# A remade order of work and a buffer of its own for batch 0's V, in attention followed by a mixer

## The chip, the cores and the metric

The kernel runs on one core of one Trainium2 chip. The metric is the device time of one execution in microseconds (us); three runs of the kernel before gave 656.35, 661.31 and 663.45, median 661.31.

## The reference

Four batches of eight heads, 576 tokens, head size 64. Queries and keys are rotated by position, scores are softmaxed and weight V; the result, 512 channels wide, goes through a token mixer of rank 32 (U, V of the mixer) and a channel mixer with a hidden width of 2048.

```python
q_rot, k_rot = rotate(q), rotate(k)
scores = q_rot @ k_rot.T / sqrt(64)
attn = exp(scores - max); attn = attn / (sum(attn) + 1e-9)
x = (attn @ v), heads side by side            # (4, 576, 512)
u = x + ((x.T @ U) @ V).T                     # mixes tokens, moe_U 576x32, moe_V 32x576
out = u + relu(u @ w_ch1) @ w_ch2             # 512x2048, 2048x512
```

The inputs come as float32; the kernel is handed the four mixer arrays as 64-bit words and turns them into float32 itself.

## The kernel before, in words

**Who decides the order.** Nothing is issued as the code reads. Every operation is recorded as a node of a `Plan`, with the nodes that it must follow. `Plan.schedule` (L321) then places all nodes on a model of the core, sorts them by the planned start, and emits them in that order; each engine's queue, and SyncE's (SP's) queue of DMA issues, runs in that order on the chip and waits at each instruction for what it needs. Every operation on the chip therefore bears the line of `emit`, L414, and this document goes by tile names.

**The planner's costs.** `cost` gives each compute instruction a duration. `transfer` (L267) gives a DMA four numbers: how long it holds the issuing queue, the delay from issue to the start of moving, how long it holds the one modelled DMA resource, and a fourth that `place` (L278) drops. `lag` (L313) gives the time from a DMA's modelled end to the start of whoever needs it. `settle` (L347) alternates a forward and a backward pass; `shaken` (L358) adds random numbers, drawn from a seed, to the due times of the nodes of one stretch and settles again. `MOVES` (L39) is a list of such shakes (seed, width, begin, length; times count back from the end). In the kernel before, a shake is kept when its planned end is earlier.

**The work.** Attention goes batch by batch, in four head pairs a batch, five query tiles a pair: 36 softmaxes a batch (in the last, half-full tile of a pair both heads share one). For each: TensorE makes the scores (tile `s`), VectorE takes the maximum (`junk`, `nb`), ScalarE the exponential (`p`) and its half-precision copy, GpSimd the low remainder (`p`), and SP issues one DMA transpose of both (`pt<-p`, or the spare buffers carved out of `room`). TensorE then multiplies with V's high part `vh`, its low part `vl` and a rotated copy `vb`. `values` (L1077) evacuates, transposes back and, after a head pair or a batch, runs `mix`.

**Loads of a batch.** `load_qk` (L907) brings K and Q of a head pair, 576 KB each, into `raw_ring` (L559), a ring of three buffers. `load_v` (L822) takes two more turns of the same ring for V, 2.5 row blocks a buffer, then squares it for a scale, splits it into `vh` and `vl`, and copies pieces within SBUF (`twice`, L892). Batch 0 therefore uses the ring in the order K, Q, V half, V half, K, Q, ...

**Weights.** `weight` (L727) loads each 1 MB group of the channel mixer's weights in two 512 KB DMAs and unpacks each in three VectorE passes (`single`, L645; tile `wt`). There are 16 loads for the first matrix and 16 for the second. The first half of batch 0 is multiplied in float32, all else in pairs of half-precision parts. The channel mixer of batch b runs beside the attention of batch b+1; for batch 3 nothing is left to run beside it.

**Constants.** `HV = 0`, so no tile takes the float32 path in which V and the weights are multiplied undivided (`plain_pv`, L819).

Of the kernel before, what the change touches and what calls it, by code (L numbers as in the profile page):

```python
# [12 lines left out]
F32 = mybir.dt.float32  # L13
# [13 lines left out]
PLAIN = HV = 0  # L27
GB = 0
# [60 lines left out]
class Plan:  # L89
# [176 lines left out]
    @staticmethod  # L266
    def transfer(calls):  # L267

        _, op, a, k = calls[0]
        out, in_ = k.get("out", a[0] if a else 0), k.get("in_", a[1] if a else 0)  # L270
        if op == "dma_start_transpose":
            return 1.37, 0.9, 1.5, 0.8
        sb = out if out.space != bass.MemoryType.DRAM else in_
        rows = list(sb.ap)[0][1]
        hw = 0.45 if rows == 128 else 0.62
        return hw, hw + 0.65, rows * free(sb) * SIZE[sb.dtype] / 335e3, 1.1
# [35 lines left out]
    @staticmethod  # L312
    def lag(a, b, turn=False):  # L313

        if a == "sync":
            return 0.8 if turn else 1.1
        if a == b:
            return {"tensor": 0.0, "scalar": 0.09, "vector": 0.127, "gpsimd": 0.1}[a]
        return LAG.get((a, b), 0.2)

    def schedule(self):  # L321
# [21 lines left out]
        for seed, width, begin, wide in MOVES:  # L343
            best = min(best, self.shaken(best, seed, width, begin, wide), key=lambda x: x[0])
# [93 lines left out]
def tile_rope_attention_then_mixer(ctx, tc, qk, v, tab, u_in, v_in, w1, w2, out):  # L438
# [63 lines left out]
    def carve(n, dtype):  # L502
# [34 lines left out]
    v32 = [  # L537
        t.rearrange("p c h w -> p c (h w)")[:, :, 0:NH * 64].bitcast(F32) if e == 0 else
        t.bitcast(F32) for e, t in enumerate((vh, vl))
    ]  # L540
# [5 lines left out]
    f = pts_.rearrange("p i n -> p (i n)").bitcast(F32)  # L546
    pt32 = [f[:, i * NC * P:(i + 1) * NC * P] for i in range(3)]
    if HV:
        pt32 += [carve(NC * P, F32) for i in range(2)]
    pt32 = cycle([x.rearrange("p (c q) -> p c q", c=NC) for x in pt32])  # L550

# [3 lines left out]
    more[2] = [x.rearrange("p (j q) -> p j q", j=NJ) for x in more[2]]  # L555
    p_rings, p16_rings, pt_rings = [
# [262 lines left out]
    def plain_pv(b, hp):  # L819
        return b == 0 and hp < HV  # L820

    def load_v(b):  # L822

        h0 = 0
        if b == 0 and HV:
            h0 = 2 * HV
            for e in range(2):
                cc = slice(e * HV * 64, (e + 1) * HV * 64)
                r = v32[e][:, :, 0:HV * 64]
                nc.sync.dma_start(  # L830
                    r[:, 0:NT, :], v[b, 0:MAIN, cc].rearrange("(c p) d -> p c d", p=P)
                )
                nc.sync.dma_start(r[0:REM, NT, :], v[b, MAIN:S, cc])
        if h0 == NH:
            return

        hn = NH - h0
        w = hn * 64
        raws = []
        for i in range(2):  # L840
            r = next(raw_ring)[:, 0:5 * w // 2]
            nc.sync.dma_start(
                r[:, 0:2 * w].rearrange("p (c d) -> p c d", c=2),
                v[b, 2 * i * P:2 * (i + 1) * P, h0 * 64:DM].rearrange("(c p) d -> p c d", p=P),
            )
            nc.sync.dma_start(
                r[0:REM, 2 * w:], v[b, MAIN:S, h0 * 64 + i * w // 2:h0 * 64 + (i + 1) * w // 2]
            )
            nc.gpsimd.memset(r[REM:P, 2 * w:], 0.0)
            raws.append(r)  # L850
        am = tmp("amv", [2], 2, f"amv{b}")

        def squares():
            for i, r in enumerate(raws):
                nc.scalar.activation(
                    out=vb.rearrange("p j h w -> p (j h w)")[:, 0:5 * w // 2], in_=r,
# [7 lines left out]
        def split(i):  # L864
            sc = state[b]["vsc"]
            parts = []
            hs = slice(h0 + i * hn // 2, h0 + (i + 1) * hn // 2)
            r = raws[i]
            if h0 == 0:
                parts.append((  # L870
                    P, vh[:, 2 * i:2 * i + 2].rearrange("p c h w -> p (c h) w")[:, :, 0:64],
                    vl[:, 2 * i:2 * i + 2].rearrange("p c (h d) -> p (c h) d", d=64),
                    r[:, 0:2 * w].rearrange("p (n d) -> p n d", d=64),
                ))
            else:
                for c in range(2):
                    parts.append((
                        P, vh[:, 2 * i + c, h0:, 0:64],
# [650 lines left out]
```

## Time and profile before

| | |
|---|---|
| runs | 656.35, 661.31, 663.45 us |
| the profiled execution's own time | 659.51 us |
| its span, first to last instruction | 657.8 us |
| busy: TensorE matmul, VectorE, ScalarE, GpSimd | 603.7, 438.3, 386.5, 224.1 us |
| bytes moved by DMA; share of the 16 engines | 92.59 MB; 65.0% |
| DMA transposes into `pt` from `p` | 130 |

The span is 1.7 us short of the execution's own time. Below, PE is TensorE, PEld its weight loads, DVE VectorE, ACT ScalarE, POOL GpSimd and SPq the issuing queue. A DMA share is the time that packets took, as a share of 16 engines; it can exceed 1.

### The profile page before, as it was taken

How to read it: one execution, taken by the hardware profiler on the slowest of the kernel's cores; microseconds unless marked ns; L12 is line 12 of the kernel's file. 1: busy time of each engine (PE TensorE's matmuls, PEld its weight loads, DVE VectorE, ACT ScalarE, POOL GpSimd, SP SyncE). 2: the span in 40 equal slices, each digit the busy share in tenths (PEclk: the TensorE clock that was granted, in tenths of full speed). 3: DMA queues.
4: the chain of work that ended last, by engine and by line, in shares of the span. 5: the costliest groups of instructions: out<-in, count | busy, mean ns of one | idle time of the engine just before them, and what ended most of it. 6: DMA issues, size and time to landing. Idle time of an engine off the chain costs nothing.

```text
span 657.8 us, 15277 instructions
## 1 busy us (share of the span) xinstructions
PE 603.7 (92%) x6005; PEld 456.5 (69%) x6005; DVE 438.3 (67%) x1094; ACT 386.5 (59%) x783; POOL 224.1 (34%) x196
## 2 busy tenths in 40 slices
PE   2776786999999989999999999999999999999997
PEld 1455464677667667777777778777776787777776
DVE  5786776999998857785787765867877644321310
ACT  4666575556788879547857775568667751220210
POOL 1655453003335545124554454054354450000000
PEclk9977687999999999999999999999999999999999
DMA  8999899989958895735879667277675771000000
GB/s 254 205 200 193 253 199 225 362 260 228 180 137 152 153 179 121 149 95 110 168 123 186 131 123 150 70 154 144 130 146 101 101 118 47 10 1 28 10 10 28
DMA packets 198057, 92.59 MB, mean 141 GB/s; under 512 B 173280, under 2 KB 186592, under 8 KB 197984
## 3 DMA queue, kind: packets, MB, share of 16 engines
q1 hardware_dynamic: 197984, 91.61, 65.0%
q8 instruction: 47, 0.77, 0.5%
q14 instruction: 26, 0.21, 0.1%
HBM read 41.70 MB, written 4.72 MB: 71 GB/s over the span
## 4 chain that ended last, share of the span: by engine, by line
PE 66%; DMA 12%; DVE 10%; ACT 7%; issue 3%; POOL 2%; SPq 1%; POOLq 0%; ACTq 0%; DVEq 0%
PE mm L414 50%; PE s L414 11%; DMA pt<-p 8%; PE pv L414 6%; ACT p L414 4%; DVE wt L414 3%; DVE junk L414 3%; DMA raw<-qk 2%; POOL p L414 1%; DVE raw L414 1%; ACT room L414 1%; ACT xf L414 1%; DMA vb<-vh 1%; DMA cs<-tab 1%; SPq L414 1%
## 5 line engine op out<-in xcount | busy, mean ns | idle before, releaser
L414 PEld LDWEIGHTS <-wt 128*128 128x128 f16 x2688 | 254.2, 98 | 74.4 <-issue 15.3
L414 POOL TENSOR_TENSOR p<-p,p 128x576 f16<-128x576 f32 x130 | 173.6, 1342 | 179.2 <-ACT p L414 139.5
L414 PE MATMUL mm<-room,wt 128*128 128x288 f16 (+1 forms) x1472 | 217.0, 297 | 0.0
L414 PE MATMUL mm<-u,wt 128*128 128x288 f16 x1344 | 183.7, 286 | 1.7 <-DVE room L414 1.5
L414 ACT ACTIVATE room<-mm 128x288 f16<-128x288 f32 (+1 forms) x128 | 52.4, 409 | 97.0 <-PE mm L414 93.0
L414 PEld LDWEIGHTS <-pt 128*128 128x128 f16 x1918 | 80.3, 101 | 35.7 <-DMA pt<-p 19.8
L414 PE MATMUL s<-qk,qk 64*128 64x288 f16 (+1 forms) x640 | 82.4, 372 | 18.7 <-DVE qk L414 11.5
L414 ACT ACTIVATE p<-p 128x576 f16<-128x576 f32 x130 | 87.2, 681 | 12.8 <-DMA pt<-p 11.2
L414 DVE SCALAR_TENSOR_TENSOR room<-mm,room 128x288 f16<-128x288 f32 x112 | 50.9, 456 | 61.5 <-ACT room L414 60.1
L414 ACT ACTIVATE p<-s,nb,bqk 128x576 f32<-128x576 f32 x72 | 59.1, 829 | 24.8 <-DVE nb L414 13.8
L414 DVE TENSOR_SCALAR_CACHE_REDUCE junk<-s,bqk 128x576 bf16<-128x576 f32 x72 | 58.0, 812 | 19.5 <-PE s L414 15.0
L414 DVE TENSOR_SCALAR_CACHE_REDUCE junk<-s 128x576 bf16<-128x576 f32 x72 | 52.2, 753 | 20.9 <-PE s L414 19.9
L414 PE MATMUL pv<-vh,pt 128*128 128x65 f16 (+1 forms) x600 | 56.3, 199 | 8.4 <-DMA pt<-p 7.5
L414 ACT ACTIVATE p<-s,nb 128x576 f32<-128x576 f32 x72 | 51.8, 738 | 19.1 <-DVE junk L414 18.2
L414 PE MATMUL pv<-vl,pt 128*128 128x64 f16 (+1 forms) x600 | 56.3, 198 | 0.3 <-DMA vl<-vl 0.3
L414 PEld LDWEIGHTS s<-qk,qk 64*128 64x128 f32 x256 | 30.2, 219 | 32.8 <-ACT p L414 14.4
L414 DVE SCALAR_TENSOR_TENSOR ob<-mm,so,x 128x288 f32<-128x288 f32 x28 | 14.4, 515 | 43.6 <-PE mm L414 43.0
L414 PE MATMUL pv<-vb,pt 128*128 128x65 f16 (+1 forms) x480 | 36.1, 198 | 2.5 <-DMA vb<-vh 2.5
L414 ACT ACTIVATE xf<-pv,rc 128x64 f32<-128x64 f32 (+1 forms) x92 | 24.8, 309 | 19.2 <-DVE rc L414 15.6
L414 DVE TENSOR_SCALAR rs<-pv,sc_v 128x2 f32<-128x2 f32 x67 | 14.5, 216 | 31.0 <-PE pv L414 30.6
L414 PE MATMUL mm<-x,wt 128*128 128x288 f32 x128 | 34.0, 421 | 1.0 <-DVE x L414 0.9
L414 DVE SCALAR_TENSOR_TENSOR wt<-wt 128x512 int32<-128x512 int32 x46 | 31.8, 722 | 0.1
(128 smaller groups left out, 653.6 us busy)
## 6 DMA issues: line engine op xcount, KB each, us to landing
raw<-qk SPq DMA_DIRECT2D x30, 576.0 KB, 4.9
wt<-w SPq DMA_DIRECT2D x23, 512.0 KB, 6.5
out_t<-ob SPq DMA_DIRECT2D x32, 144.0 KB, 2.1
raw<-vt SPq DMA_DIRECT2D x8, 512.0 KB, 4.6
x<-w SPq DMA_DIRECT2D x6, 512.0 KB, 5.9
vb<-vh SPq DMA_DIRECT2D x8, 264.0 KB, 6.8
pt<-p SPq DMA_TRANSPOSE x130, 3.4
u<-w SPq DMA_DIRECT2D x3, 512.0 KB, 4.5
```

Source lines behind the costliest of these rows:

```text
L414: getattr(getattr(nc, eng), op)(*a, **k)
```

## The change

1. `transfer` and `lag` get other constants. For a transpose: issue 1.37 to 1.42 us, delay 0.9 to 0.95, moving 1.5 to 1.75, lag to the consumer 0.8 to 1.3. For an ordinary DMA: issue 0.45 to 0.55 (0.62 to 0.65 with fewer rows than 128), delay on top of it 0.65 to 0.55, 335 to 320 GB/s, lag 1.1 to 1.7.
2. `MOVES` is another list of about as many shakes, and each is now applied whatever its planned end.
3. V of batch 0 gets a buffer `v0` of its own, loaded by three DMAs (512, 512 and 128 KB) in place of two of 512 and two of 64 KB, so `raw_ring` is used by K and Q alone in batch 0. Its low parts are made on VectorE only, and one fill replaces two.
4. The float32 path is now chosen by a set of tiles, `PLT`, which is empty; its spare buffers move into `room` and no instruction uses them.

```diff
-            return 1.37, 0.9, 1.5, 0.8
+            return 1.42, 0.95, 1.75, 0.55
...
-        hw = 0.45 if rows == 128 else 0.62
-        return hw, hw + 0.65, rows * free(sb) * SIZE[sb.dtype] / 335e3, 1.1
+        hw = 0.55 if rows == 128 else 0.65
+        return hw, hw + 0.55, rows * free(sb) * SIZE[sb.dtype] / 320e3, 0.9
...
-            return 0.8 if turn else 1.1
+            return 1.3 if turn else 1.7
...
-            best = min(best, self.shaken(best, seed, width, begin, wide), key=lambda x: x[0])
+            best = self.shaken(best, seed, width, begin, wide)
...
+    v0 = cst.tile([P, NC, DM], F32, name="v0")
...
+        if b == 0:
+            for i in range(2):
+                r = v0[:, 2 * i:2 * i + 2]
                 nc.sync.dma_start(
...
+            nc.sync.dma_start(v0[0:REM, NT], v[b, MAIN:S])
+            fill(v0[REM:P, NT], 0.0)
+            whole = v0.rearrange("p c d -> p (c d)")
+            raws = [
+                (whole[:, 0:5 * DM // 2], v0[:, 0:2], v0[0:REM, NT, 0:DM // 2]),
+                (whole[:, 5 * DM // 2:], v0[:, 2:4], v0[0:REM, NT, DM // 2:]),
+            ]
+        for i in range(0 if b == 0 else 2):
+            r = next(raw_ring)[:, 0:5 * DM // 2]
...
-                scaled_low(lo, x, sc[:n], hi, "DP")
+                scaled_low(lo, x, sc[:n], hi, "DP" if b else "D")
```

## Rows read from the trace of the kernel before

**Rows 1.** The page's span in 40 equal slices, busy tenths.
```profile
PE   2776786999999989999999999999999999999997
...
DMA  8999899989958895735879667277675771000000
```
**Rows 2.** Windows: length, busy us (instructions) by engine, granted clock, DMA share, GB/s.
```profile
0.00:11.00 11.00, 0.08 (x2) 0.08 (x2) 5.54 (x17) 3.29 (x3) 1.97 (x10) 1.00 0.74 241
...
120.00:200.00 80.00, 78.00 (x438) 57.40 (x439) 76.37 (x141) 54.58 (x112) 18.29 (x14) 1.00 0.81 220
200.00:554.00 354.00, 345.20 (x4018) 264.53 (x4016) 250.47 (x686) 241.08 (x481) 151.31 (x134) 1.00 0.68 131
554.00:657.80 103.80, 100.47 (x822) 79.86 (x818) 26.61 (x60) 16.01 (x36) 0.00 (x0) 1.00 0.04 15
```
**Rows 3.** The same view of the stretch 11 to 120 us, whole and cut.
```profile
11.00:120.00 109.00, 79.91 (x733) 54.63 (x733) 79.32 (x194) 71.52 (x153) 52.57 (x39) 0.83 1.02 222
...
11.00:30.00 19.00, 13.10 (x75) 8.35 (x75) 13.06 (x32) 12.48 (x19) 9.40 (x6) 1.00 0.98 228
30.00:60.00 30.00, 22.43 (x254) 16.07 (x252) 23.25 (x63) 21.75 (x47) 17.91 (x13) 0.87 1.05 189
60.00:90.00 30.00, 23.05 (x170) 15.40 (x172) 20.73 (x46) 15.63 (x33) 13.69 (x12) 0.62 0.98 235
90.00:120.00 30.00, 21.33 (x238) 14.82 (x238) 22.29 (x57) 21.66 (x56) 11.57 (x9) 0.89 1.08 239
```
**Rows 4.** TensorE's waits, 11 to 50 us: total us, times, longest.
```profile
PE pv L414 <- DMA vb<-vh: 2.5, 1, 2.5
...
PE mm L414 <- DVE amv L414: 1.6, 1, 1.6
```
**Rows 5.** TensorE's waits, 50 to 125 us.
```profile
PE s L414 <- ACT p L414: 5.0, 6, 2.3
```
**Rows 6.** TensorE's waits, 125 to 300 us and then 300 to 660 us.
```profile
PE pv L414 <- DMA pt<-p: 4.3, 7, 1.2
...
PE pv L414 <- DMA pt<-p: 2.8, 5, 1.1
```
**Rows 7.** The chain that ended last, 205 to 246 us: start, length, what.
```profile
216.86 4.84 DMA pt<-p
...
238.96 5.12 DMA pt<-p
```
**Rows 8.** SP's queue in order of time, 0 to 45 us: start, length, issue.
```profile
3.61 5.89 SPq L414 DMA_DIRECT2D raw<-vt  x4
10.89 0.35 SPq L414 DMA_DIRECT2D raw<-qk  x1
...
26.38 0.57 SPq L414 DMA_DIRECT2D raw<-qk  x1
```
**Rows 9.** DMA issues up to 109 us: count, size, median us to landing.
```profile
wt<-w SPq DMA_DIRECT2D x10, 512.0 KB, 5.5
raw<-qk SPq DMA_DIRECT2D x6, 576.0 KB, 4.8
...
pt<-p SPq DMA_TRANSPOSE x22, 3.4
...
pt<-room SPq DMA_TRANSPOSE x7, 3.8
room<-room SPq DMA_TRANSPOSE x7, 4.2
```
**Rows 10.** SP's queue at 335 us, four transposes.
```profile
335.05 8.07 SPq L414 DMA_TRANSPOSE pt<-p  x4
```
**Rows 11.** Windows of transposes alone, and of weight loads alone.
```profile
335.00:343.00 8.00, 8.00 (x115) 6.49 (x114) 6.54 (x19) 4.36 (x6) 5.04 (x5) 1.00 0.86 114
...
122.00:126.00 4.00, 3.94 (x17) 2.76 (x16) 4.00 (x9) 2.19 (x6) 0.00 (x0) 1.00 1.05 372
```
**Rows 12.** VectorE's groups up to 120 us: busy us, mean ns of one.
```profile
L414 DVE SCALAR_TENSOR_TENSOR vl<-raw,sc_v,vh 64x256 f16<-64x256 f32 (+1 forms) x4 | 4.4, 1104 | 0.0
```

More of the change, by code (lines that the diff above doesn't have):

```diff
@@ L27 @@
 PLAIN = HV = 0
+PLT = set()
 GB = 0
@@ L535, in tile_rope_attention_then_mixer @@
     vb = cst.tile([P, NJ - NC, NH, HW], F16, name="vb")
[L537 to L540, printed above, removed]
+    v0 = cst.tile([P, NC, DM], F32, name="v0")
     p_all = [cst.tile([P, S], F32, name=f"p{i}") for i in range(3)]
@@ L545, in tile_rope_attention_then_mixer @@
     pt_all = [pts_[:, i].rearrange("p (j q) -> p j q", j=NJ) for i in range(4)]
[L546 to L550, printed above, removed]
     more = [[carve(n, d) for _ in range(k)] for n, d, k in (
@@ L555, in tile_rope_attention_then_mixer @@
     more[2] = [x.rearrange("p (j q) -> p j q", j=NJ) for x in more[2]]
+    pt32 = [carve(NC * P, F32) for i in range(3)]
+    pt32 = cycle([x.rearrange("p (c q) -> p c q", c=NC) for x in pt32])
     p_rings, p16_rings, pt_rings = [
@@ L817, in tile_rope_attention_then_mixer, with plain_pv @@
     ready = {}
-    def plain_pv(b, hp):
-        return b == 0 and hp < HV
+    def plain_pv(b, hp, t):
+        return b == 0 and (hp, t) in PLT
     def load_v(b):
[L824 to L829, printed above, removed]
+        raws = []
+        if b == 0:
+            for i in range(2):
+                r = v0[:, 2 * i:2 * i + 2]
                 nc.sync.dma_start(
-                    r[:, 0:NT, :], v[b, 0:MAIN, cc].rearrange("(c p) d -> p c d", p=P)
+                    r, v[b, 2 * i * P:2 * (i + 1) * P].rearrange("(c p) d -> p c d", p=P)
@@ L832, in load_v @@
                 )
[L833 to L841, printed above, removed]
+            nc.sync.dma_start(v0[0:REM, NT], v[b, MAIN:S])
[5 more added lines that the diff above has]
+            ]
@@ L842, in load_v @@
+        for i in range(0 if b == 0 else 2):
+            r = next(raw_ring)[:, 0:5 * DM // 2]
             nc.sync.dma_start(
-                r[:, 0:2 * w].rearrange("p (c d) -> p c d", c=2),
-                v[b, 2 * i * P:2 * (i + 1) * P, h0 * 64:DM].rearrange("(c p) d -> p c d", p=P),
+                r[:, 0:2 * DM].rearrange("p (c d) -> p c d", c=2),
+                v[b, 2 * i * P:2 * (i + 1) * P].rearrange("(c p) d -> p c d", p=P),
             )
             nc.sync.dma_start(
-                r[0:REM, 2 * w:], v[b, MAIN:S, h0 * 64 + i * w // 2:h0 * 64 + (i + 1) * w // 2]
+                r[0:REM, 2 * DM:], v[b, MAIN:S, i * DM // 2:(i + 1) * DM // 2]
@@ L848, in load_v @@
             )
-            nc.gpsimd.memset(r[REM:P, 2 * w:], 0.0)
-            raws.append(r)
+            nc.gpsimd.memset(r[REM:P, 2 * DM:], 0.0)
+            raws.append((
+                r, r[:, 0:2 * DM].rearrange("p (c d) -> p c d", c=2), r[0:REM, 2 * DM:]
+            ))
         am = tmp("amv", [2], 2, f"amv{b}")
         def squares():
-            for i, r in enumerate(raws):
+            for i, (r, _, _) in enumerate(raws):
                 nc.scalar.activation(
-                    out=vb.rearrange("p j h w -> p (j h w)")[:, 0:5 * w // 2], in_=r,
+                    out=vb.rearrange("p j h w -> p (j h w)")[:, 0:5 * DM // 2], in_=r,
@@ L865, in split @@
             sc = state[b]["vsc"]
[L866 to L870, printed above, removed]
+            hs = slice(i * NH // 2, (i + 1) * NH // 2)
+            _, x, rest = raws[i]
+            parts = [
+                (
                     P, vh[:, 2 * i:2 * i + 2].rearrange("p c h w -> p (c h) w")[:, :, 0:64],
                     vl[:, 2 * i:2 * i + 2].rearrange("p c (h d) -> p (c h) d", d=64),
[L873 to L878, printed above, removed]
-                        vl[:, 2 * i + c, h0 * 64:].rearrange("p (h d) -> p h d", d=64),
-                        r[:, c * w:(c + 1) * w].rearrange("p (n d) -> p n d", d=64),
-                    ))
-            parts.append((
-                REM, vh[0:REM, NT, hs, 0:64],
-                vl[0:REM, NT, hs.start * 64:hs.stop * 64].rearrange("p (h d) -> p h d", d=64),
-                r[0:REM, 2 * w:].rearrange("p (n d) -> p n d", d=64),
-            ))
+                    x.rearrange("p c (h d) -> p (c h) d", d=64),
+                ),
+                (
+                    REM, vh[0:REM, NT, hs, 0:64],
+                    vl[0:REM, NT, hs.start * 64:hs.stop * 64].rearrange("p (h d) -> p h d", d=64),
+                    rest.rearrange("p (h d) -> p h d", d=64),
+                ),
+            ]
             for n, hi, _, x in parts:
@@ L889, in split @@
             for n, hi, lo, x in parts:
-                scaled_low(lo, x, sc[:n], hi, "DP")
+                scaled_low(lo, x, sc[:n], hi, "DP" if b else "D")
         def twice():
-            hh, cols = slice(h0, NH), slice(h0 * 64, DM)
-            nc.sync.dma_start(vh[REM:P, NT, hh, :], vh[0:P - REM, 0, hh, :])
-            nc.sync.dma_start(vl[REM:P, NT, cols], vl[0:P - REM, 0, cols])
-            nc.sync.dma_start(vb[REM:P, :, hh, :], vh[0:P - REM, 1:NC, hh, :])
-            nc.sync.dma_start(vb[0:REM, :, hh, :], vh[P - REM:P, 0:NT, hh, :])
-        if b < 2 and (b == 0 or h0 or HV):
-            heads = slice(h0, NH) if b == 0 else slice(0, min(2 * HV, NH))
-            fill(vh[:, :, heads, 64:HW], 1.0)
+            nc.sync.dma_start(vh[REM:P, NT], vh[0:P - REM, 0])
+            nc.sync.dma_start(vl[REM:P, NT], vl[0:P - REM, 0])
+            nc.sync.dma_start(vb[REM:P], vh[0:P - REM, 1:NC])
+            nc.sync.dma_start(vb[0:REM], vh[P - REM:P, 0:NT])
+        if b == 0:
+            fill(vh[:, :, :, 64:HW], 1.0)
         squares()
@@ L1029, in score_tiles, with softmax_tile @@
         return ss
-    def softmax_tile(b, hp, s, dst, sm):
+    def softmax_tile(b, hp, t, s, dst, sm):
         with plan.sooner(20 if b == 0 else 50):
             p = next(p_rings[b > 0])
-            plain = plain_pv(b, hp)
+            plain = plain_pv(b, hp, t)
             parts = [(half(s, n), p[:, n * HS:(n + 1) * HS]) for n in range(2)]
@@ L1057, in softmax_tile @@
                 nc.scalar.activation(out=o, in_=i, func=AF.Exp, bias=nb[0], scale=down, **more)
-        if plain_pv(b, hp):
+        if plain_pv(b, hp, t):
             for j in range(NC):
@@ L1077, in values @@
     def values(b, hp, t, pts, sm):
-        plain = plain_pv(b, hp)
+        plain = plain_pv(b, hp, t)
         pv = next(pv_rings[b > 0])
@@ L1089, in values @@
                         mm.append((o[:, f if t == NT else 0, 0:64], pt[:k, j, :],
-                                   v32[f][:k, j, hp * 64:(hp + 1) * 64]))
+                                   v0[:k, j, (2 * hp + f) * 64:(2 * hp + f + 1) * 64]))
             else:
@@ L1235, in tiles @@
                 sm = tmp("sm", [2], 5, "")
-                if t == NT and plain_pv(b, hp):
+                if t == NT and plain_pv(b, hp, t):
                     fill(sm[:, 1:2], 1.0)
                 for e, s in enumerate(score_tiles(b, hp, t)):
-                    pt = next(pt32 if plain_pv(b, hp) else pt_rings[b > 0])
-                    softmax_tile(b, hp, s, pt, sm[:, e:e + 1])
+                    pt = next(pt32 if plain_pv(b, hp, t) else pt_rings[b > 0])
+                    softmax_tile(b, hp, t, s, pt, sm[:, e:e + 1])
                     pts.append(pt)
```

80 rows, old and new, of the table MOVES are left out of this document.

## The prediction

> **What bounds the kernel now.** Read the slices first: TensorE is at nine tenths or more from the eighth slice to the last but one, and only the first seven, some 115 us, leave room, where the DMA engines stand at eight to nine tenths nearly throughout [rows 1]. The windows then give sizes. From 120 to 554 us TensorE is busy 423.2 of 434 us at full clock, and from 554 us on it runs the last batch's channel mixer with next to no other work, 100.5 of 103.8 us [rows 2]. From 11 to 120 us, batch 0's attention, it is busy 79.9 of 109 us, while the DMA share is 1.02 [rows 3]. So idle time of TensorE is 11 us at the start, 29.1 in batch 0's attention, 10.8 from 120 to 554 and 3.3 at the end, 54 in all; the rest is matmuls, of which the change touches none.
>
> Within the stretch of 29.1 us the granted clock is also low: 0.87, 0.62 and 0.89 of full in its three later parts, a mix of the levels 1.2 and 2.4 GHz, after stretches in which TensorE idled a quarter of the time [rows 3]. Matmul time lost to it: 22.43 x 0.13 + 23.05 x 0.38 + 21.33 x 0.11 = 14.0 us. The most that an order could win there is thus 43 us, if the DMA engines allow it.
>
> Do they? Four transposes were issued in 8.07 us [rows 10], and the window that holds them and little else has a share of 0.86 [rows 11]: 8 x 0.86 / 4 = 1.72 us of all 16 engines each. Up to 109 us there are 22 + 7 + 7 = 36 of them [rows 9], 62 us. A 512 KB weight load takes 0.524 MB / 372 GB/s = 1.41 us at the pace of the window of loads alone [rows 11]; ten were issued ahead of the last transpose [rows 9], 14 us. K, Q and V of batch 0 and the tables (0.6 + 4.7 + 1.2 + 0.7 MB) take another 20 us. That is 96 us, and with the start the whole stretch: the DMA engines, not a late engine, set the length of batch 0's attention. The Trainium skill says otherwise in "DMA: Bandwidth & Descriptors", section "Latency and other measured facts": a DMA transpose moves 261 GB/s. By that, as an estimate, one of 295 KB would take 1.13 us, 36 of them 41 us, the engines would have 21 us to spare, and the most that the order could win below would be nearer; the trace, with 114 GB/s at a share of 0.86, does not agree.
>
> **The change, part by part.** The sum is against the profiled execution, 659.5 us, which is 1.8 below the median.
>
> *V's own buffer.* SP's issue of V holds for 5.89 us, because its second half takes the ring buffer that K of the first pair still occupies; K of the second pair follows at 10.89 and Q, which needs V's first buffer back, at 26.38 us [rows 8]. Afterwards V goes out without a wait, and K of the second pair can follow straight behind it. The DMA share up to 11 us is 0.74 [rows 2], so at most 0.26 x 11 = 2.9 us of transfer time is unused, and some 1.7 of that lie ahead of the first packet. TensorE waits for V twice: 1.6 us for its scale and 2.5 for the rotated copy [rows 4]. Gain between 0 and 4.1; I take 1.5, nearest to the 1.2 us of transfer time. The transfers only swap places beyond that. One DMA issue and one fill fewer: nothing, SP and POOL wait there anyway. Low parts on VectorE alone: nothing, all four of batch 0 run there already [rows 12]. The float32 path and its buffers: no instruction.
>
> *Later landings, from 120 us on.* A transpose was planned at 0.9 + 1.5 + 0.8 = 3.2 us from issue to consumer, and will be at 0.95 + 1.75 + 1.3 = 4.0. On the chain its length is 4.84 and 5.12 us from the producer's end [rows 7], so the old plan was some 1.6 us short there and the new one is 0.8 better. TensorE's waits for transposes there are 7 of 4.3 us and 5 of 2.8 [rows 6], 7.1 in all, 0.59 us on average, 1.2 at most: 0.8 us covers most of them if other matmuls are moved up, and TensorE has them, since the channel mixer runs beside. I take 5 of 7.1. If the new order only opens other gaps the term is 0; as a re-drawn order it might lose as much as it wins, -5.
>
> *The order of batch 0's attention.* The planner now books 1.75 instead of 1.5 us of DMA for each of 36 transposes, 9 us more in this stretch, and so sees it as full. A weight load that goes behind the last transpose instead of ahead of it ends the attention 1.41 us sooner; one more ahead of it, 1.41 later. Bounds: all ten behind, +14.1; the six that remain of the first sixteen ahead, -8.5. But each load needs three VectorE passes, and VectorE is busy 76.4 of 80 us from 120 to 200 [rows 2], so few can go there. I take two: 3 us, near the middle. What is late next in this stretch: the exponentials, 5.0 us of waits for ACT [rows 5].
>
> *Loads landing later* (1.7 instead of 1.1 us of lag): the plan for K and Q of 576 KB goes from about 4.0 to 4.6 us, and the trace has 4.8 [rows 9]; from 120 us on hidden under matmuls, before that part of the term above.
>
> Sum: 1.5 + 5 + 3 = 9.5; 659.5 - 9.5 = 650.0, and with 1.8 for the median **652 us**.
>
> **The rivals.** *No change to be measured.* The stretch to 120 us is filled by bytes that stay, and the removed waits of 7.1 us come back as waits for ACT or POOL. For it: the DMA share of 1.02. Against: the planned landings were short by a measured amount. Only V's 1.5 us remain: 660.
>
> *Slower.* Place: SP's queue and the DMA engines between 60 and 110 us. A plan with later landings issues loads earlier; what stands behind the last transpose now (six first weights, then V, K and Q of batch 1) goes ahead of it, while TensorE has only batch 0's attention to do. Price 1.41 us a load; five eat the 6.5 us of the other two terms, and from ten on the kernel is slower by more than 1%. Twelve: 659.5 - 6.5 + 17 + 1.8 = 672. For it: the share is full there, so every load displaces a transpose. Against: the planner now books the transposes at their measured cost.
>
> *Much faster.* Half of the ten loads go behind (7 us), and TensorE, with shorter gaps, gets back half of the 14.0 us of slow clock: 1.5 + 5 + 7 + 7 = 20.5, 641. Against: VectorE after 120 us, and the DMA arithmetic above.
>
> **How the numbers follow.** Chances: the forecast 0.38 (its own range 645 to 656), no change 0.32, slower 0.18, much faster 0.12. About 1%, 6.6 us, is what a measurement of this kernel tells from no change. Faster by over 1% (under 654.7): 0.38 + 0.12 = 0.50; within: 0.32; slower: 0.18. The range, 641 to 667, leaves out half of the much faster case and most of the slower one.
>
> **What would show it.** In the profile after: (1) SP issues V without a hold and the second pair's K before 8 us; the DMA share up to 11 us is above 0.8. (2) TensorE's waits for transposes after 125 us total about 2 us instead of 7.1. (3) The last transpose of batch 0 is issued some 3 us or more before 108 us, with eight or fewer weight loads ahead of it; slower if there are fifteen or more. (4) Busy TensorE from 120 to 554 us at 98% or above. The prediction is wrong if the granted clock before 120 us moves by more than a tenth either way, if VectorE makes TensorE wait between 120 and 200 us, or if the re-drawn order opens gaps after 200 us that were not there.

## The result, and the profile after

The changed kernel took 666.45 us (median of 13 runs, 663.58 to 668.78), the kernel before 660.32 (13 runs): ratio 1.0088, 95% interval 1.0064 to 1.0113. It is slower by 6 us where 8 us less was forecast. The profiled execution took 666.45 us, its span is 664.7 against 657.8, its mean granted clock 0.964 against 0.971.

Slices of the page after, TensorE and DMA [rows 1]:

```profile
PE   2476877899999999999999999999999999999997
...
DMA  9898998986994899726869767159576671000000
```

Windows after, columns as in [rows 2, 3]:

```profile
0.00:11.00 11.00, 0.39 (x2) 0.39 (x4) 6.10 (x15) 2.84 (x4) 1.89 (x11) 1.00 0.83 299
11.00:120.00 109.00, 76.31 (x684) 51.94 (x683) 74.14 (x180) 67.51 (x138) 52.26 (x41) 0.79 0.90 188
11.00:30.00 19.00, 10.06 (x31) 5.55 (x31) 12.63 (x28) 12.43 (x20) 7.27 (x6) 1.00 0.93 222
30.00:60.00 30.00, 19.80 (x249) 14.03 (x245) 20.95 (x51) 20.05 (x43) 19.98 (x15) 0.96 0.97 176
60.00:90.00 30.00, 22.14 (x163) 14.97 (x163) 19.96 (x43) 14.09 (x33) 9.81 (x9) 0.56 0.84 217
90.00:120.00 30.00, 24.31 (x246) 17.39 (x247) 20.61 (x59) 20.95 (x44) 15.21 (x12) 0.73 0.88 150
120.00:200.00 80.00, 75.94 (x403) 54.63 (x402) 71.11 (x136) 50.10 (x110) 10.82 (x9) 0.99 0.86 253
200.00:554.00 354.00, 348.58 (x4028) 269.51 (x4026) 252.19 (x689) 245.05 (x488) 176.86 (x152) 1.00 0.70 133
```

The DMA engines are busier than before in the first 11 us (0.83 for 0.74) and idler in all of batch 0's attention (0.90 for 1.02), while TensorE does less there (76.31 for 79.91 us, 684 matmuls for 733) and at a lower clock from 60 to 120 us (0.56 for 0.62, then 0.73 for 0.89). From 200 to 554 us TensorE is busier than before (348.58 for 345.20).

TensorE's waits after, 11 to 50 us, then 50 to 125, then 125 to 300, then 300 to 660 [rows 4 to 6]:

```profile
PE s L409 <- ACT p L409: 14.1, 9, 3.6
...
PE s L409 <- ACT p L409: 7.0, 6, 2.4
PE s L409 <- DVE qk L409: 2.7, 1, 2.7
...
PE pv L409 <- DMA pt<-p: 1.9, 4, 0.6
...
PE pv L409 <- DMA pt<-p: 1.7, 3, 0.8
```

The waits for transposes behind 125 us have halved, 3.6 for 7.1. The new waits are early, and they are for the exponentials (`p`), not for a transfer: 14.1 us from 11 to 50 us, where before had

```profile
PE s L414 <- ACT p L414: 2.8, 2, 1.8
```

SP's queue after, whole stretch to 120 us [rows 8, 9]:

```profile
4.08 2.10 SPq L409 DMA_DIRECT2D v<-vt  x3
...
8.30 0.35 SPq L409 DMA_DIRECT2D raw<-qk  x1
...
50.53 0.68 SPq L409 DMA_DIRECT2D raw<-qk  x1
...
70.88 3.44 SPq L409 DMA_DIRECT2D wt<-w  x6
...
115.59 1.31 SPq L409 DMA_TRANSPOSE pt<-p  x1
```

The weight loads up to then, and the last transpose of batch 0 before:

```profile
wt<-w SPq DMA_DIRECT2D x9, 512.0 KB, 6.8
```

```profile
108.48 1.30 SPq L414 DMA_TRANSPOSE pt<-p  x1
```

V goes out without a hold, and the load at 8.30 us is Q of the second pair, whose K went ahead of V. But the last transpose of batch 0 is issued at 115.59 us, 7.1 later than before (108.48), with nine weight loads ahead of it, one fewer. The load at 50.53 us is Q of the third head pair, which before left at 37.83.

Where the time is lost shows in milestones read from the timelines: TensorE's start of the third pair's scores, of the token mixers (tile `gt`) of batch 0's two halves and of batches 1 to 3, and the end, in us from the start of the span:

| | 3rd pair | mix, half 1 | mix, half 2 | batch 1 | batch 2 | batch 3 | end |
|---|---|---|---|---|---|---|---|
| before | 54.6 | 66.7 | 118.2 | 276.5 | 414.6 | 550.6 | 657.8 |
| after | 60.0 | 73.0 | 126.1 | 284.5 | 419.2 | 557.1 | 664.7 |
| r1 (below) | 58.8 | 69.1 | 120.4 | 275.2 | 410.8 | 545.4 | 652.8 |
| r3 (below) | 57.2 | 72.7 | 125.7 | 278.0 | 413.5 | 549.0 | 656.3 |

In the changed kernel 7.9 us are lost by the second mix of batch 0, as much as the whole kernel loses (6.9), and 5.4 of them are gone by the third pair's first scores. A late second mix alone doesn't cost the time, though: r3 is 7.5 us late there and ends 1.5 us ahead of before, so what stands behind it counts as well. The page's busy times divide the 6.9 another way: TensorE 607.5 for 603.7 us busy, 3.8 more for the same matmuls, and 3.1 us more idle. The scores alone carry 4.7 of busy time, at a lower clock. Page's groups, after and before, 640 score matmuls each (busy us, mean ns, idle before):

```profile
L409 PE MATMUL s<-qk,qk 64*128 64x288 f16 (+1 forms) x640 | 87.1, 380 | 30.9 <-ACT p L409 17.4
```

```profile
L414 PE MATMUL s<-qk,qk 64*128 64x288 f16 (+1 forms) x640 | 82.4, 372 | 18.7 <-DVE qk L414 11.5
```

### The profile page after: what moved, and what is told of

Read it like the earlier page. It is cut to its first block, busy times and chain, and to the rows that moved or that the text cites. A ratio compares the mean times of both kernels' runs of the same rounds, so it can differ in the third digit from the quotient of the medians.

```text
span 664.7 us, 15258 instructions
## 1 busy us (share of the span) xinstructions
PE 607.5 (91%) x6005; PEld 459.7 (69%) x6005; DVE 432.9 (65%) x1080; ACT 382.4 (58%) x776; POOL 241.8 (36%) x212
## 4 chain that ended last, share of the span: by engine, by line
PE 70%; DVE 9%; DMA 7%; ACT 4%; issue 3%; POOL 1%; POOLq 0%; SPq 0%; ACTq 0%; DVEq 0%
PE mm L409 53%; PE s L409 11%; PE pv L409 7%; DMA pt<-p 5%; ACT p L409 3%; DVE wt L409 2%; DVE junk L409 2%; DVE qk L409 1%; DVE raw L409 1%; DMA u<-w 1%; POOL p L409 1%; DVE u L409 1%; DMA room<-room 1%; ACT room L409 1%; DMA pt<-room 0%
## 5 line engine op out<-in xcount | busy, mean ns | idle before, releaser
L409 PE MATMUL mm<-u,wt 128*128 128x288 f16 x1344 | 180.8, 286 | 3.2 <-DVE u L409 1.2
L409 PE MATMUL s<-qk,qk 64*128 64x288 f16 (+1 forms) x640 | 87.1, 380 | 30.9 <-ACT p L409 17.4
L409 PEld LDWEIGHTS <-pt 128*128 128x128 f16 x1918 | 82.2, 101 | 22.6 <-issue 7.8
L409 PEld LDWEIGHTS s<-qk,qk 64*128 64x128 f32 x256 | 31.9, 227 | 47.5 <-ACT p L409 26.1
L409 ACT ACTIVATE xf<-pv,rc 128x64 f32<-128x64 f32 (+1 forms) x85 | 23.1, 310 | 23.4 <-DVE rc L409 22.8
```

The costliest lines, as they stand in the source:

```text
L409: getattr(getattr(nc, eng), op)(*a, **k)
```

## The experiments

In every kernel marked as an order written out, the planner is replaced by a literal list of the order and of the engine chosen for each operation, and nothing else differs from the program named:

```diff
     def schedule(self):
-        best = self.settle(sorted(range(len(key)), key=lambda n: key[n]), 7)
-        for seed, width, begin, wide in MOVES:
...
+        self.order = struct.unpack(f"<{len(raw) // 2}H", raw)
+        self.chosen = {n: w[0][ways[n]] for n, w in enumerate(self.nodes)}
```

The theory to begin with: the re-drawn order of batch 0's attention costs the time and the rest of the order gains. The rival: V's buffer costs it, or the rest does.

### The order cut at the first channel-mixer matmul, and the buffer alone

**e1**: the changed program in the whole order of before (`ORDER` = before's). 

> The changed program (V of batch 0 in its own buffer), emitted in the order and with the engine choices of the kernel before. If the remade order is the cause of the loss, the time is that of before, 660 us (659 to 661.5). If the buffer itself is the cause (its loads, its single fill), it is 665 to 667.

663.85 us, ratio 1.0047 [1.0027, 1.0068], between the two expectations: in an order made for the ring the buffer costs about 3 us.

**e2**: the changed program, `ORDER` = before's up to the channel mixer + the changed from there. 

> The changed program; the 471 operations that the kernel before planned ahead of its first channel-mixer matmul stand in before's order, all others in the changed order. If the loss lies wholly in batch 0's attention, the first channel-mixer matmul comes at 111 us as before, the rest keeps the 0.5 us that the changed order won after that point, and the time is 659 to 660. If it lies in the order of the rest, 665 or more.

659.39, ratio 0.9980 [0.9962, 0.9998]: the time as expected, though the first channel-mixer matmul comes at 114.1 us and not at 111.

**e3**: the mirror, `ORDER` = the changed first + before's from there. 

> The mirror image: the 468 operations that the changed kernel planned ahead of its first channel-mixer matmul in the changed order, all others in before's. If the loss lies wholly in batch 0's attention, 666 to 668 with the first channel-mixer matmul at 118 us; if in the rest, 660.

670.21, ratio 1.0144 [1.0121, 1.0167]: slower than the 666 to 668 expected, since it also misses what the changed rest gains.

**e7**: the program of before (V in the ring), `ORDER` cut as in e2. 

> The program of the kernel before (V of batch 0 in the ring) with before's order up to its first channel-mixer matmul and the changed order behind it. If the three effects add (buffer +3.3, first stage +7, rest -4), this has the -4 alone: 655.5 to 657.5, faster than both. If what the rest wins is only a late first stage caught up, 660.

656.98, ratio 0.9949 [0.9925, 0.9974]: faster than both kernels, and 2.4 us under e2, which differs from it by the buffer.

The four add up. The changed first part costs 666.45 - 659.39 = 7.1 us before the changed rest, and 670.21 - 663.85 = 6.4 before the old one. The changed rest gains 4.5 and 3.8. So the rest did nearly what was forecast, and two things ahead of 120 us ate it: the order there (6.4 to 7.1) and the buffer (2.4 to 3.3 in orders made for the ring).

### Why the buffer costs

**e5**: as e1, but the squares of V are cut where its loads are cut. 

> The run with before's order and V in its own buffer (663.85 us), with one edit: V's two squares on ScalarE are cut where its loads are cut, blocks 0 and 1 in the first, blocks 2 to 4 in the second, so the first no longer waits for the second load. There the first square began at 12.27 us after 3.59 us of waiting for V, in the kernel before at 10.16. If that wait is what the buffer costs, the first square begins near 10.5 and the time returns to 660 to 661.5; if the cost lies elsewhere (K of the second pair beside V in the DMA engines, the rest of the ring), it stays at 663 to 664.5.

```diff
-                (whole[:, 0:5 * DM // 2], v0[:, 0:2], v0[0:REM, NT, 0:DM // 2]),
-                (whole[:, 5 * DM // 2:], v0[:, 2:4], v0[0:REM, NT, DM // 2:]),
+                (whole[:, 0:2 * DM], v0[:, 0:2], v0[0:REM, NT, 0:DM // 2]),
+                (whole[:, 2 * DM:], v0[:, 2:4], v0[0:REM, NT, DM // 2:]),
```

ScalarE's first square of V in e1, then in e5 (start, length, instruction, idle ahead of it):

```profile
12.27 1.27 ACT L477 ACTIVATE vb<-v 128x1280 f16<-128x1280 f32 x1 [3.59 <-DMA v<-vt]
```

```profile
10.65 1.06 ACT L477 ACTIVATE vb<-v 128x1024 f16<-128x1024 f32 x1 [2.39 <-DMA v<-vt]
```

662.66 us, ratio 1.0035 [1.0009, 1.0061]. The changed code kept the halves of 2.5 row blocks that fitted the ring; in its own buffer V comes in loads of 2, 2 and 1, so the first square spans two loads. Cutting it along the loads recovers 1.2 of the 3.3 us by the medians; the intervals of e1 and e5 overlap, and where the other 2 us go was not found.

**e4**: the changed order, V's loads, squares and scale pulled forward in it. 

> The changed order with V of batch 0 pulled forward: its three loads go ahead of K of the second pair, its two squares on ScalarE ahead of the first exponential, and the scale that follows from them ahead of the unpacking of the mixer's U on VectorE. Nothing else moves. If the late V (first V multiplication at 35 us, before at 22.6) is what cost batch 0's attention its 7 us, the time falls to 660 to 663. If the loss is spread over the whole order of that stage, it stays at 665 to 667.

667.77, ratio 1.0106 [1.0088, 1.0124]: the theory missed. V came sooner and nothing else did, so the late V is not what holds up batch 0 in the changed order.

### Where batch 0 loses its 7 us

**e6**: the changed order, Q of the third pair loaded right behind its K and rotated some 13 us earlier (`ORDER` with these nodes moved). 

> The changed order with batch 0's third pair pulled forward: its Q is loaded right behind its K (at about 29 us, not 50.5), and its rotation on VectorE stands about 13 us earlier. Theory: the third pair's first scores, at 60.0 us against 54.6 before, are late because that load stands behind the transposes on SP's queue; then they come at 56 to 57 and the time falls to 662 to 664. Rival: the stage is bound by its DMA or by its exponentials all along; then they come at 59 to 60 and the time stays at 665.5 to 667.

664.26, ratio 1.0060 [1.0033, 1.0087]: 2 us back by the medians, with intervals that overlap those of the changed kernel. In the changed kernel the rotation of that Q is on the chain, as VectorE shows (start, length, instruction):

```profile
55.95 2.23 DVE L409 TENSOR_TENSOR raw<-raw,csq 128x1152 f32<-128x1152 f32 x1
58.21 1.71 DVE L409 TENSOR_TENSOR qk<-raw 128x576 f32<-128x576 f32 x1
```

and TensorE starts the pair's scores at 59.98, after 2.72 us of waiting for `qk`. VectorE has no idle time ahead of the rotation, so it is VectorE's own work that ends last there, and not the load. In e6 the pair begins no sooner (62.5, where 56 to 57 was expected): the second pair now ends later.

**e8**: `ORDER` = before's up to the second pair's first scores. 

> The changed program (V in its own buffer) with the order of before up to the second head pair's first scores of batch 0, and the changed order from there on. Theory, the slip is spread over the pairs: in the changed kernel the second pair's first score step starts 1.6 us later than before (37.0 against 35.4 us), the third's 5.4 us later (60.0 against 54.6), the first channel-mixer matmul 7.4 us later (118.6 against 111.2). If each pair's piece of the order makes its own share, this kernel gets back about 1.6 us of the changed kernel's time: 664.9 us, the first mixer matmul at about 117. Rival, the first pair's order starts a chain that the later pairs only carry on: then nearly all of the 6 to 7 us comes back, 659 to 661 us and the first mixer matmul at 111 to 113.

667.79, ratio 1.0092 [1.0058, 1.0126].

**e9**: `ORDER` = before's up to the third pair's first scores. 

> As the kernel before it, but with the order of before up to the third head pair's first scores of batch 0. Theory, spread over the pairs: 5.4 of the 7.4 us of slip are there by the third pair's first scores, so about 5 us come back: 661 us, with the first mixer matmul at 113 to 114. Rival, it is one decision in the third or fourth pair: then little comes back, 665 us and the first mixer matmul at 117 or later.

666.84, ratio 1.0086 [1.0059, 1.0113].

**e10**: `ORDER` = before's up to the first token mixer. 

> The changed program with the order of before up to and including the first token-mixer step of batch 0 (it starts at 66.7 us before and at 73.0 in the changed kernel), and the changed order from there on. From that step to the first channel-mixer matmul both kernels need nearly the same time (44.5 us before, 45.6 in the changed kernel). Theory, the whole slip is made ahead of that step: it starts at 67 to 70 us, the channel mixer at 112 to 115, and the time is within 2 us of the kernel with the order of before to the channel mixer (659.4). Rival, the changed order loses the time again in the second half of batch 0: the mixer at 117 or later and 664 to 667 us, as with the cuts at the second and third pair.

664.83, ratio 1.0062 [1.0034, 1.0090]; the mixer of half 1 starts at 67.0 us, as before, and yet the first channel-mixer matmul at 117.8.

Neither theory got its numbers: no cut short of the channel mixer recovers more than 1.6 us. One reason is of the method. A splice puts a weight load of the changed order, issued there at 24.47 us, behind the prefix, while its unpacking stays ahead of other VectorE work. VectorE's waits, 50 to 80 us, in e9 and then e10:

```profile
DVE wt L477 <- DMA wt<-w: 3.1, 1, 3.1
```

```profile
DVE wt L477 <- DMA wt<-w: 2.6, 1, 2.6
```

So e9 and e10 carry a wait that neither parent has, and they don't locate the loss cleanly. TensorE's second step of the third pair's scores, which stands behind the mix of half 1, in before, e10 and the changed kernel:

```profile
70.56 2.20 PE L414 MATMUL s<-qk,qk 64*128 64x288 f32 x8
```

```profile
75.33 2.95 PE L477 MATMUL s<-qk,qk 64*128 64x288 f32 x8 [4.41 <-DVE x L477]
```

```profile
76.19 2.95 PE L409 MATMUL s<-qk,qk 64*128 64x288 f32 x8
```

In e10 TensorE waits here for `x`, which VectorE makes behind that unpacking, and is 4.8 us late where the mix of half 1 was still on time. From this step to the second mix the three need 47.6, 50.0 and 49.9 us. So in the changed kernel 5.6 of the 7.9 us are lost ahead of 76 us, and 2.3 behind it.

For these 2.3 us the changed kernel itself shows something, 80 to 100 us, after and then before:

```profile
80.00:100.00 20.00, 14.89 (x77) 9.58 (x79) 11.78 (x28) 13.19 (x23) 9.34 (x8) 0.50 0.85 163
```

```profile
80.00:100.00 20.00, 16.35 (x172) 11.06 (x169) 15.99 (x46) 15.44 (x34) 13.22 (x11) 0.84 1.04 190
```

The changed order has 77 matmuls there, at 1.2 GHz throughout (granted 0.50); before has 172, at 0.84. VectorE's waits, 60 to 120 us, after and before, show what is left when the other matmuls are gone: scores, their maximum, the exponential, the next scores, one behind the other.

```profile
DVE junk L409 <- PE s L409: 13.4, 8, 2.5
```

```profile
DVE junk L414 <- PE s L414: 5.2, 7, 1.4
```

That TensorE's own scores become the wait of VectorE is a loop, not a bound: the matmuls that would fill it (values of the pair before, mixer steps) stand elsewhere in the order. It is made again in e8, e9 and e10 (78 to 80 matmuls in that stretch). It stands in r3 too (below), so it doesn't make a kernel slow by itself, and which decisions of the order lose the 5.6 us ahead of it was not isolated.

### The constants, with no shakes

The changed program with `MOVES = ()`, in the four combinations of the sets of constants of `transfer` and of `lag`:

```diff
-            return 1.42, 0.95, 1.75, 0.55
+            return 1.37, 0.9, 1.5, 0.8
...
-            return 1.3 if turn else 1.7
+            return 0.8 if turn else 1.1
```

**p1**, old moving, old lag: 

> The changed program (V in its own buffer) planned without any shake, with all planner constants of before. One of four: the constants for issue, delay and moving (the moving set) and those for the lag to the consumer (the lag set), each old or new. Theory: the new moving set, 1.75 us of one DMA resource for a transpose, makes batch 0 look bound by transfers, and the third pair's Q is put behind transposes; so the first channel-mixer matmul comes at 109 to 113 us with the old moving set and at 115 to 120 with the new, whatever the lag. Rival: the longer lag does it, or the shakes did and the four do not differ by 3 us. Here: 109 to 113 by the theory; TensorE's waits for transposes after 125 us 6 us or more; whole time 670 to 685, since the shakes are missing.

**p2**, old moving, new lag: 

> As above with the new lag set alone. Theory: first channel-mixer matmul at 109 to 114 us, TensorE's waits for transposes after 125 us 2 to 4 us. Rival (the lag delays batch 0): 115 or later.

**p3**, new moving, old lag: 

> As above with the new moving set alone. Theory: first channel-mixer matmul at 115 to 120 us, third pair's first scores at 58 us or later, waits for transposes after 125 us 5 us or more. Rival: 109 to 113 us.

**p4**, both new: 

> As above with both new sets, which is the changed kernel without its shakes. Theory: first channel-mixer matmul at 116 to 121 us, waits for transposes after 125 us 2 to 4 us. If the shakes made batch 0 late, 110 to 113 here.

| | us (2 runs) | ratio, 95% | mix, half 2 | first channel-mixer matmul |
|---|---|---|---|---|
| p1 | 683.59 | 1.0322 [1.0268, 1.0375] | 118.4 | 111.1 |
| p2 | 672.90 | 1.0160 [1.0114, 1.0207] | 118.7 | 112.2 |
| p3 | 684.48 | 1.0335 [1.0267, 1.0403] | 119.1 | 111.5 |
| p4 | 676.51 | 1.0215 [1.0162, 1.0268] | 123.7 | 115.8 |

Later landings gain 8 to 11 us in bare plans. The new moving times gain nothing (0.9 and 3.6 us slower, the first within the runs' spread), and only both together start the channel mixer late, in one trace each: the theory, that the moving set does it whatever the lag, missed in p3 (111.5, where 115 to 120 was forecast). TensorE's waits for transposes after 125 us fall from 11.7 to 3.2 us (p1 to p2) and from 6.3 to 3.0 (p3 to p4).

### The same search for everybody

Does the list of shakes or do the constants make the loss? Four kernels had their order searched alike: both kernels' lists and then a long search of further random shakes, each kept only if the planned end came earlier (the rule of before). The better of two such searches was written out. The constants worked in the search alone; each kernel holds only the order that came of it, so one kernel stands for each set of constants.

**r0**, the control: program and constants of before. 

> The program and all planner constants of before, with as long a new search of shakes by planned end as the two searches with later landings had. Theory, the later landings made the gain of 7 us there and not the search: this kernel stays within 2 us of before (659 to 663 us) and TensorE's waits for transposes after 125 us stay near the 7.1 us of before. Rival, the search itself made it: 653 to 656 us.

660.68, ratio 0.9995 [0.9972, 1.0018]: the longer search alone gives nothing.

**r1**: program of before, searched with the new `lag` alone (1.3 for 0.8 after a transpose, 1.7 for 1.1 after any other DMA). 

> The program of before (V in the ring), planned with the new later landings and the old (unremeasured) moving times, its order taken from a new search of shakes by the same rule as the change's. Theory, the remeasured moving times made the late first stage: the first mixer matmul comes at 110 to 113 us, TensorE's waits for transposes after 125 us sum to 2 to 3 us, and the time is 652 to 657 us, as good as the mixture of the two orders (656.98) or better. Rival, the late first stage is what the new search by the mean end gives with any constants: first mixer matmul at 115 or later and 660 to 665 us.

**653.95 us** (651.65 to 657.23, 6 runs), ratio 0.9881 [0.9850, 0.9913]: the fastest kernel here, 12.5 us under the changed one. TensorE's waits from 125 us on, r0 and then r1:

```profile
PE pv L476 <- DMA pt<-p: 7.1, 11, 1.7
```

```profile
PE pv L476 <- DMA pt<-p: 2.4, 5, 1.0
```

With the later landings the waits are 4.7 us shorter, and r1 is 6.7 us under r0; time, waits and first channel-mixer matmul (112.8) are as the theory said. Its windows, columns as in [rows 2]:

```profile
11.00:120.00 109.00, 80.37 (x724) 55.29 (x725) 81.14 (x198) 69.03 (x140) 51.27 (x40) 0.84 0.97 217
...
120.00:200.00 80.00, 78.58 (x448) 57.46 (x448) 76.31 (x145) 53.94 (x114) 17.86 (x12) 1.00 0.83 232
200.00:554.00 354.00, 348.74 (x4059) 269.19 (x4058) 252.04 (x688) 243.71 (x495) 155.76 (x133) 1.00 0.69 130
```

Batch 0 is nearly as good as before (80.37 us busy for 79.91, its second mix 2.2 us later), and from 120 to 554 us TensorE is busy 427.3 us for 423.2.

**r2**: as r1, searched with the new moving times too. 

> The same program and the same search of shakes, with both new sets of constants (later landings and remeasured moving times). Theory: the first mixer matmul comes at 113 to 117 us and the time is 3 to 6 us above the kernel with the old moving times. Rival, the moving times do not matter once the order is shaken: the same time within 2 us.

658.34, ratio 0.9939 [0.9917, 0.9962]: 4.4 us above r1, as forecast, though only 0.8 of it is in the first channel-mixer matmul (113.6 for 112.8).

**r3**: the changed program with all its constants, only the list differs from the changed kernel. 

> The changed program (V of batch 0 in its own buffer) with both new sets of constants, and the same long search of shakes kept by planned end, where the changed kernel keeps its own list. Theory, V's buffer together with the remeasured moving times makes the late first stage, whatever list of shakes is taken: the first channel-mixer matmul comes at 115 us or later and the time is 3 us or more above the same search with V in the ring (658.34): 661 to 667 us. Rival, the changed kernel's list made it: the mixer at 111 to 114 us and 657 to 660 us.

657.82, ratio 0.9953 [0.9930, 0.9975]. The theory had the late mixer right (117.8 us) and the time wrong; the rival the reverse. The same program with the same constants runs 8.6 us faster in another order. V's buffer, planned for, shows no cost against the ring (r2), one search against one.

In the milestones r3 is as late as the changed kernel at the second mix, 125.7 for 126.1, and then makes most of it up in one go: it is 6.5 us ahead at batch 1's mix, 5.7 at batch 2's, 8.1 at batch 3's. From 126 to 280 us, after and then r3:

```profile
126.00:280.00 154.00, 147.63 (x1231) 109.32 (x1231) 132.27 (x295) 110.28 (x228) 56.84 (x43) 1.00 0.83 191
```

```profile
126.00:280.00 154.00, 150.42 (x1314) 112.97 (x1313) 133.56 (x295) 116.56 (x244) 58.27 (x43) 1.00 0.84 198
```

2.8 us less idle there; the rest of the 6.1 won up to batch 1's mix is not accounted for. No single wait is behind it: the longest that TensorE has from 125 to 300 us in the changed kernel is 0.9 us.

## Why the prediction was wrong, point by point

**The order of batch 0's attention: the step that failed.** "The DMA engines, not a late engine, set the length of batch 0's attention", and the 1.41 us for each weight load that hang on it, don't hold. With one weight load fewer ahead of the last transpose, that transpose left 7.1 us later, while the share fell to 0.90. In r2 seven go ahead of it, three fewer than before with all other transfers the same, and it leaves 3.6 us later than before where the price says 4.2 sooner:

```profile
wt<-w SPq DMA_DIRECT2D x7, 512.0 KB, 6.0
```

```profile
112.05 1.32 SPq L476 DMA_TRANSPOSE pt<-p  x1
```

+3 was forecast, -6.4 to -7.1 measured (e1 against e3, e2 against the changed kernel), inside the bound of -8.5 but by another mechanism. No run takes a load out of before's own order, so how much room that order leaves is not shown.

The sum to 96 us went wrong at its first price, 1.72 us a transpose from a share of 0.86 over 8 us. The window moved 0.91 MB, which is three transposes of 295 KB and not four, and two of its microseconds are

```profile
337.00:338.00 1.00, 1.00 (x10) 0.79 (x9) 0.98 (x5) 0.50 (x2) 0.39 (x1) 1.00 2.17 109
339.00:340.00 1.00, 1.00 (x11) 0.80 (x9) 0.23 (x2) 0.32 (x1) 0.00 (x0) 1.00 1.22 270
```

The share is 2.17 where 109 GB/s move and 1.22 where 270 do: it adds up the times of packets that are under way together, and near 1 it doesn't tell what room is left. A low share does, as in r3, 80 to 100 us:

```profile
80.00:100.00 20.00, 14.92 (x79) 8.81 (x80) 12.15 (x28) 12.36 (x22) 10.24 (x9) 0.54 0.55 104
```

Here the share is 0.55, and batch 0 is as late as ever. What holds these twenty microseconds is the chain of scores, maximum and exponential with few other matmuls between; what loses the time ahead of them stays open, with waits for exponentials (14.1 for 2.8 us) as the largest sign. The Trainium skill, cited in the prediction ("DMA: Bandwidth & Descriptors", "Latency and other measured facts", 261 GB/s for a DMA transpose), was set aside there for the 114 GB/s of the whole window. The 270 GB/s of 339 to 340 us, with transposes alone under way, don't speak against it.

**V's own buffer.** +1.5 was forecast; -3.3 in before's order (e1), about 0 where the order was planned for it (r3 against r2, one search each). All three signs came about: no hold, K of the second pair before 8 us, 0.83. They were signs of earlier transfers, and not of V: in the changed kernel that K went ahead of it, and ScalarE's first square moved from 10.16 us to 12.27 in e1 and, behind an exponential, to 15.10 in the changed order. Before and after:

```profile
10.16 1.27 ACT L414 ACTIVATE vb<-raw 128x1280 f16<-128x1280 f32 x1 [1.55 <-DMA raw<-vt]
```

```profile
15.10 1.25 ACT L409 ACTIVATE vb<-v 128x1280 f16<-128x1280 f32 x1
```

The lower end of "Gain between 0 and 4.1" rested on no row.

**Later landings: right.** Forecast 5 of 7.1 us; 3.8 to 4.5 measured in the changed rest (e3 to after, e1 to e2), which has the new moving times and the new list as well, and 6.7 in a whole order (r0 to r1). The waits went to 3.6, 2.4 in r1, about 2 said.

**The clock.** The slow matmul time, worked out as the prediction did: 19.80 x 0.04 + 22.14 x 0.44 + 24.31 x 0.27 = 17.1 us for 14.0. From 90 to 120 us the clock fell from 0.89 to 0.73, more than the tenth that was named as a sign of error, though over 11 to 120 us it moved only from 0.83 to 0.79. TensorE at 98% from 120 to 554 us was missed narrowly: (75.94 + 348.58) / 434 = 97.8%.

**The rivals.** "Slower" had the right sign, with the wrong mechanism (no twelve loads went ahead, nine did) and mostly the wrong place: of the 7.9 us 5.4 were lost ahead of the 60 to 110 us that it named. That 666.45 us still lies within the stated 641 to 667 is luck: the upper end reaches into this rival, and its mechanism didn't happen. The mishap that came was named only as a side remark: the order was re-drawn, and a re-drawn stretch "might lose as much as it wins". That remark was priced behind 120 us alone, where the draw won. It should have been a term for batch 0, of both signs.

**Left open.** Which decisions of the changed order lose the time ahead of 76 us, and which start the loop of 80 to 100 us; where 2 us of the buffer's cost go; and how much of the 6.7 us (r0 to r1) and of the 4.4 (r1 to r2) is the luck of the draw, since each is one search against another. For the later landings the bare plans point the same way twice.

## To carry to other kernels

A busy share of the DMA engines near 1 doesn't say that they set a stage's length: look for what waits last, and test with one transfer fewer. When a planner's constants and its search list change together, the outcome is a new draw; search alike with each set of constants, with a control, before crediting either. Here the two landing times at the consumer (`lag`) gave the best order found, 1.2% under before, and the rest of the change, moving times, buffer and list together, took more than that back.

## What was not expected of the hardware

Twelve runs of one kernel in one sitting spread by 6 to 7 us (r0 657.97 to 664.29, e1 659.17 to 666.53), so a single profiled execution can stand 5 us off its median, as e1's does (659.17 against 663.85). And the clock came back late in the changed kernel: from 90 to 100 us TensorE was busy 8.75 of 10 us, and the granted clock was still 0.50 (1.2 GHz).

```profile
80.00:90.00 10.00, 6.14 (x31) 3.83 (x31) 6.35 (x15) 6.32 (x12) 5.02 (x4) 0.50 0.78 187
90.00:100.00 10.00, 8.75 (x47) 5.76 (x49) 5.43 (x14) 6.86 (x12) 4.32 (x4) 0.50 0.93 138
```

What came ahead of it was a stretch with 6.14 of 10 us; in the kernel before the same ten us (90 to 100) were granted in full.
